# Adding and transposing transfers that wait for each other, in a convolution, row norm and feed-forward kernel whose order a planner writes

## The chip, the core and the metric

The kernel runs on one core of a Trainium2 chip. The metric is the device time of one execution in microseconds (us), lower is better: the median of three executions. A profile comes from one more execution. The engines are TensorE (PE, matrix products; PEld, its weight loads), VectorE (DVE), ScalarE (ACT), GpSimd (POOL) and SyncE (SP, which here only issues transfers). Sixteen DMA engines move data; transfers are issued from the queues of SP, POOL and, at the start, ACT.

## What is computed

The input x is 8 sequences of 4224 tokens of 192 numbers. First each token gets, for each of 8 heads, a softmax over 7 weights, and the weighted sum of itself and the six tokens ahead of it; then a row norm; then two products with a ReLU between; and the sum with the convolution's result is the output. In the reference's words, shortened:

```python
w = exp(weight_gen - max(weight_gen, -1)); w = w / (sum(w, -1) + 1e-09)
x_unf = x_pad[:, arange(S)[:, None] + arange(K)[None, :], :].reshape(B, S, K, H, group)
y = einsum('bshk,bskhg->bshg', w, x_unf).reshape(B, S, D)
mu = mean(y, -1); var = mean((y - mu) ** 2, -1)
yn = (y - mu) / sqrt(var + 1e-06) * g_ln
out = y + maximum(yn @ w_ch1, 0.0) @ w_ch2        # 192 -> 768 -> 192
```

## The kernel before

The 33792 tokens lie as 128 partitions of 264 tokens each. They are worked off in chunks of 4 or 6 tokens a partition (convolution), in parts of 4, 8 or 12 (row norm) and in groups of 4 (products): 51 chunks, 29 parts, 66 groups.

Softmax of a stretch: maxima on VectorE, subtraction on GpSimd (L333), exponentials on ScalarE, sums and the weights' product on VectorE into the PSUM tile wn.

Convolution of a chunk, `conv`: VectorE makes the seven products of x and wn, two taps at a time into tiles `pr` (five of them) and one into `y` (L395). Two of the `pr` tiles are then added up, half to half, by a transfer that accumulates in SBUF, issued from GpSimd: `dma_add` (L401), the *adding* transfer, 102 in all. GpSimd sums the rest into y with four additions (`add`, L398).

Row norm of a part, `norm`: ScalarE makes the sums and squares (L439, L444) and the root, VectorE a Newton step (L472 to L478), ScalarE the scaled rows `xh` (L490). For each group of 4 tokens ScalarE writes the fp16 half of xh into `hl` (L506) and GpSimd the rest of the split (L508). SP then issues a transposing transfer from `hl` into `xT` (L512), 66 in all: the *transposing* transfer. There are two hl tiles and three xT tiles; ScalarE may write an hl again when the transposing transfer that reads it has landed, and SP may issue the next transposing transfer into an xT when TensorE has read the one before.

Products of a group: three units of 256 hidden channels, each with 16 wide products and its share of the narrow ones, with which two units fill one stretch (L522); ScalarE evicts with a ReLU (L552), VectorE makes the low half (L554); 72 products of the second layer (L591 to L593) follow and VectorE adds them to y (L604). SP stores y (L611), and loads x (L302) and the softmax weights (L308).

Nothing of this is ordered by a scheduler at run time. `Plan.order` lists all operations once: each has an engine, a planned cost, operations that it depends on, and a due time `want` (its token, less a number from the table WANT). It picks, among the engines, the operation that may start earliest, with operations that are due first preferred within AHEAD ns, and none that is due more than WINDOW after the oldest that is left. Transfers share one planned pipe (`dma_free`), with a cost of their own each: `dma=3300.0 * n / 6` for an adding one, 2700 for a transposing one, and `dma_ns` for the rest. Each engine then runs its own list strictly in that order. An instruction that waits holds everything behind it on its engine, and on SP and GpSimd that goes for transfers' issues too.

Of the kernel before, what the change touches and what calls it, by code (L numbers as in the profile page):

```python
# [12 lines left out]
ALU = mybir.AluOpType  # L13
# [3 lines left out]
P = 128  # L17
# [6 lines left out]
CHUNK = 6  # L24
# [4 lines left out]

WANT = {'load': 38.75, 'wload': 44.01, 'max': 26.33, 'sub': 29.98, 'exp': 31.81, 'sum': 24.37,  # L30
    'rcp': 22.57, 'inv': 22.65, 'mul': 24.16, 'conv': 21.21, 'step': 0.73, 'dma': -2.14, 'add':
    -1.02, 'sums': 11.85, 'squares': 7.05, 'rstd': 13.07, 'newton': 9.37, 'xh': 6.82, 'lo':
    11.91, 'relu': 3.64, 'hlo': 0.84, 'narrow': 3.27, 'o0': -2.91, 'o1': -4.07, 'o2': -3.07,
    'o3': -3.06, 'final': -0.48}
W_WANT = {'load': 35.41, 'a': 15.24, 'c': 21.99, 's1': 17.87, 'load2': 9.56, 'c2': 13.77, 's2':
    3.7}
FIRST = {'soft': 1.2, 'conv': 7.09, 'norm': 7.75}
AHEAD = 58.5
WINDOW = 12.5

# [8 lines left out]
class Op:  # L49
    __slots__ = ("rank", "eng", "cost", "want", "fn", "lat", "dma", "deps", "nxt", "left", "ready",  # L50
                 "bufs", "start", "end")


class Plan:
# [10 lines left out]

    def op(self, eng, cost, want, fn, r=(), w=(), lat=120.0, dma=0.0):


        o = Op()
        o.rank, o.eng, o.cost, o.want, o.fn, o.lat, o.dma = len(self.ops), eng, cost, want, fn, lat, dma  # L70
        o.deps, o.nxt, o.ready, o.start, o.end = set(), [], 0.0, None, None
        o.bufs = []
        for k in (*r, *w):
# [17 lines left out]
    def order(self):  # L91
        tenant = {p: [None] * len(t) for p, t in self.pools.items()}
        free, cand, dma_free, out = {}, {}, 0.0, []
        for o in self.ops:
            o.left = len(o.deps)
            for d in o.deps:
                d.nxt.append(o)
            cand.setdefault(o.eng, [])
            free[o.eng] = 0.0
            if not o.left:  # L100
                cand[o.eng].append(o)
# [10 lines left out]
        def earliest(o):  # L112
            t = max(free[o.eng], o.ready)
            for b in o.bufs:
                if b.slot is None:
                    v = vacant(b) if b.ops[0] is o else None
                    if v is None:
                        return None
                    t = max(t, v[0])
            return t  # L120

        by_want, lead = sorted(self.ops, key=lambda o: o.want), 0
        while len(out) < len(self.ops):
# [21 lines left out]
            if o.dma:  # L145
                dma_free = max(t + o.cost + self.DMA_START[o.eng], dma_free) + o.dma
                o.end = dma_free + self.DMA_END
            cand[o.eng].remove(o)
            for x in o.nxt:
# [9 lines left out]
def kernel(  # L159
# [72 lines left out]
    def dma_ns(n):  # L232
        return n * P / 280.0

# [43 lines left out]

    def sp(want, fn, r, w, dma):
        op("SP", 450, want, fn, r=r, w=w, dma=dma)  # L280

# [79 lines left out]
    def conv(c):  # L361
# [38 lines left out]
        def dma_add(to, k):  # L400
            Q.dma_start(flat(to), flat(k), accum_op=ALU.add, max_dma_last_dim=CHUNK * D * 4)  # L401

# [13 lines left out]
        for i, k in enumerate((1, 3)):  # L416
            op("Pool", 900, c0 + 2 * i * st + WANT["dma"], lambda k=k: dma_add(k, k + 1), [(prs[k], 1)],
               [(prs[k], 0)], dma=3300.0 * n / 6)
        for i, (k, h) in enumerate(((5, 0), (5, 1), (1, 0), (3, 0))):
# [9 lines left out]
    def norm(pa):  # L429
# [53 lines left out]
        for g in range(0, n, NT):  # L483
# [18 lines left out]
            def pairs(xh):  # L502
# [9 lines left out]
               lambda hl=hl, xT=xT: SY.dma_start_transpose(at(xT), at(hl).rearrange("p t a d -> p (t a d)")),  # L512
               [(hl, 0), (hl, 1)], [xT], 2700.0)

# [283 lines left out]
    for t in range(NT):  # L798
        output(prev, t, C - WANT[f"o{t}"])
    for o in plan.order():  # L800
        o.fn()

# [29 lines left out]
```

## Time and profile before

| | |
|---|---|
| median of 3 executions | 920.84 us (918.64 to 921.96) |
| the profiled execution | 925.24 us, its span 923.5 us |
| mean granted clock of TensorE | 0.979 of 2.4 GHz |
| busy: PE, DVE, POOL, ACT | 824.6, 789.4, 696.9, 674.8 us |
| transfers on SP's queue | 47.6% of the 16 DMA engines' span |
| transfers on GpSimd's queue | 31.5% |
| waits of ScalarE's hl (L506) for xT's transfer | 23.4 us, 4 times, at most 12.3 |

The span runs from the first instruction to the last; the profiled execution's own time has 1.74 us around it. An engine's busy time is that of its instructions, DMA issues of SP and semaphores not among them. The clock is the share of TensorE's cycles that was granted: 1.0 is 2.4 GHz, and its other level is 1.2 GHz, so 0.9 over a stretch means that it was at the lower level for a fifth of it. The DMA share is the mean of 16 engines and can pass 1 in a stretch, since a packet counts where it starts. "To landing" runs from a transfer's issue to its last byte.

### The profile page before, as it was taken

How to read it: one execution, taken by the hardware profiler on the slowest of the kernel's cores; microseconds unless marked ns; L12 is line 12 of the kernel's file. 1: busy time of each engine (PE TensorE's matmuls, PEld its weight loads, DVE VectorE, ACT ScalarE, POOL GpSimd, SP SyncE). 2: the span in 40 equal slices, each digit the busy share in tenths (PEclk: the TensorE clock that was granted, in tenths of full speed). 3: DMA queues.
4: the chain of work that ended last, by engine and by line, in shares of the span. 5: the costliest groups of instructions: out<-in, count | busy, mean ns of one | idle time of the engine just before them, and what ended most of it. 6: DMA issues, size and time to landing. Idle time of an engine off the chain costs nothing.

```text
span 923.5 us, 21518 instructions
## 1 busy us (share of the span) xinstructions
PE 824.6 (89%) x8716; PEld 734.4 (80%) x8716; DVE 789.4 (85%) x833; ACT 674.8 (73%) x1773; POOL 696.9 (75%) x403
## 2 busy tenths in 40 slices
PE   0047898999999999999999995999999999899997
PEld 0036786988888898879989885988889888789997
DVE  6998997999999989999999895898989989774442
ACT  2687785897968788878886884878787789487421
POOL 3798997999879888797797793889779788783100
PEclk9989998999999999999999997999999999899999
DMA  9966869998997988996989879879988876951411
GB/s 225 225 116 140 204 137 153 186 180 162 195 189 146 176 180 143 173 186 158 192 129 207 183 106 124 196 159 142 199 170 137 182 167 124 114 124 47 78 53 53
DMA packets 137995, 142.23 MB, mean 154 GB/s; under 512 B 107495, under 2 KB 108903, under 8 KB 137895
## 3 DMA queue, kind: packets, MB, share of 16 engines
q1 hardware_dynamic: 122983, 88.95, 47.6%
q0 software_dynamic: 14688, 51.91, 31.5%
q8 instruction: 68, 1.11, 0.6%
q14 instruction: 32, 0.26, 0.1%
q10 hardware_dynamic: 224, 0.00, 0.0%
HBM read 36.43 MB, written 25.95 MB: 68 GB/s over the span
## 4 chain that ended last, share of the span: by engine, by line
DVE 29%; PE 25%; ACT 8%; POOL 7%; DMA 6%; issue 6%; DVEq 0%; POOLq 0%; ACTq 0%
DVE pr L395 14%; PE ph L522 12%; DVE hlo L554 7%; DMA xT<-hl 6%; POOL y L398 5%; PE po L591 4%; PE po L593 4%; PE po L592 4%; DVE y L395 2%; DVE y L604 2%; ACT hh L552 2%; ACT xh L490 2%; ACT junk L439 2%; ACT hl L506 1%; POOL hl L508 1%
## 5 line engine op out<-in xcount | busy, mean ns | idle before, releaser
L398 POOL TENSOR_TENSOR y<-y,pr 128x1152 f32<-128x1152 f32 (+1 forms) x204 | 498.7, 2469 | 72.6 <-DVE pr L395 69.3
L591 PE MATMUL po<-c_w2h,hh 128*128 128x192 f16 x1584 | 391.6, 247 | 0.0
L593 PE MATMUL po<-c_w2h,hlo 128*128 128x192 f16 x1584 | 391.1, 247 | 0.0
L592 PE MATMUL po<-c_w2l,hh 128*128 128x192 f16 x1584 | 391.1, 247 | 0.0
L522 PE MATMUL ph<-xT,c_w1h 128*128 128x256 f16 x2376 | 333.0, 277 | 37.6 <-DMA xT<-hl 20.3
L395 DVE TENSOR_TENSOR pr<-x,wn 128x2304 f32<-128x2304 f32 (+1 forms) x153 | 338.4, 2217 | 4.8 <-DMA x<-in_x_dram 2.6
L522 PEld LDWEIGHTS <-c_w1h 128*128 128x128 f16 x2376 | 230.2, 99 | 78.0 <-issue 41.7
L554 DVE SCALAR_TENSOR_TENSOR hlo<-ph,hh 128x1024 f16<-128x1024 f32 x198 | 238.9, 1219 | 55.0 <-ACT hh L552 54.6
L552 ACT ACTIVATE hh<-ph 128x1024 f16<-128x1024 f32 x198 | 200.0, 1012 | 94.5 <-PE ph L522 61.1
L522 PE MATMUL ph<-xT,c_w1l 128*128 128x256 f16 (+1 forms) x1584 | 214.3, 277 | 16.3 <-DVE hlo L554 16.0
L591 PEld LDWEIGHTS <-hh 128*128 128x128 f16 x1584 | 155.5, 98 | 12.4 <-issue 10.7
L508 POOL TENSOR_TENSOR hl<-xh,hl 128x768 f16<-128x768 f32 x66 | 113.2, 1715 | 60.7 <-ACT hl L506 60.3
L592 PEld LDWEIGHTS <-hh 128*128 128x128 f16 x1584 | 155.6, 98 | 1.9
L593 PEld LDWEIGHTS <-hlo 128*128 128x128 f16 x1584 | 155.6, 98 | 0.1
L522 PEld LDWEIGHTS <-c_w1l 128*128 128x128 f16 (+1 forms) x1584 | 109.6, 97 | 51.3 <-issue 31.4
L490 ACT ACTIVATE xh<-y,s 128x192 f32<-128x192 f32 x264 | 123.9, 536 | 31.0 <-DVE s L478 31.0
L444 ACT ACTIVATE junk<-y,s 128x192 f32<-128x192 f32 x264 | 119.3, 452 | 6.1
L401 POOL DMA_DIRECT2D pr<-pr x102 | 97.5, 964 | 28.8 <-DVE pr L395 26.3
L604 DVE SCALAR_TENSOR_TENSOR y<-po,c_fs,y 128x384 f32<-128x384 f32 x132 | 80.4, 611 | 44.1 <-PE po L593 44.0
L439 ACT ACTIVATE junk<-y 128x192 f32<-128x192 f32 x264 | 95.2, 361 | 29.2 <-POOL y L398 23.1
L506 ACT ACTIVATE hl<-xh 128x768 f16<-128x768 f32 x66 | 54.9, 832 | 23.5 <-DMA xT<-hl 23.4
L395 DVE TENSOR_TENSOR y<-x,wn 128x1152 f32<-128x1152 f32 (+1 forms) x51 | 60.3, 1182 | 0.3
(62 smaller groups left out, 333.3 us busy)
## 6 DMA issues: line engine op xcount, KB each, us to landing
pr<-pr POOLq DMA_DIRECT2D x60, 576.0 KB, 6.7
x<-in_x_dram SPq DMA_DIRECT2D x30, 576.0 KB, 8.5
out_dram<-y SPq DMA_DIRECT2D x30, 576.0 KB, 4.5
pr<-pr POOLq DMA_DIRECT2D x42, 384.0 KB, 6.4
out_dram<-y SPq DMA_DIRECT2D x21, 384.0 KB, 4.6
x<-in_x_dram SPq DMA_DIRECT2D x20, 384.0 KB, 8.5
w<-in_weight_gen_dram SPq DMA_DIRECT2D x21, 336.0 KB, 8.4
pr<-in_moe_w_ch_dram SPq DMA_DIRECT2D x1, 1152.0 KB, 7.2
```

Of the source, the lines that this page charges most:

```text
L395: V.tensor_tensor(out=ov, in0=xv, in1=wv, op=ALU.mult)
L398: E.tensor_tensor(out=flat(0), in0=flat(0), in1=flat(k), op=ALU.add)
L439: A.activation(junk, at(y)[:, j, :], AF.Identity, scale=-1.0 / D, accum_out=at(s4)[:, 3, t : t + 1])
L444: A.activation(junk, at(y)[:, j, :], AF.Square, bias=at(s4)[:, 3, t : t + 1], accum_out=at(s4)[:, 0, t : t + 1])
L490: A.activation(at(xh)[:, t, :], at(y)[:, i, :], AF.Identity, bias=at(s4)[:, 3, g + t : g + t + 1], scale=at(s4)[:, 1, g + t : g + t + 1])
L508: lambda xh=xh, hl=hl: Q.tensor_tensor(out=halves(hl, True), in0=pairs(xh), in1=halves(hl, False), op=ALU.subtract),
L522: T_.matmul(at(gp["ph"][u])[:, r, v * 2 * P : (v + 1) * 2 * P], W[w][rows, wb, (2 * u + v) * P : (2 * u + v + 1) * P], xv[rows, r, xb, :, ...
L552: lambda: A.activation(at(hh)[:, us, :], at(ph), AF.Relu), [ph], [(hh, u)])
L554: lambda: V.scalar_tensor_tensor(out=at(hlo)[:, us, :], in0=at(ph), scalar=0.0, in1=at(hh)[:, us, :], op0=ALU.max, op1=ALU.subtract),
L591: T_.matmul(o, tok(hh, j), w2h[:, j, :], start=(j == 0), stop=False)
L592: T_.matmul(o, tok(hh, j), w2l[:, j, :], start=False, stop=False)
L593: T_.matmul(o, tok(hlo, j), w2h[:, j, :], start=False, stop=(j == NF - 1))
```

## The change

Two kinds of transfers are marked: the adding ones ("add") and the transposing ones ("turn"). In the plan, a transfer of one kind starts no sooner than the planned end of the last one of the other kind; and in the program it waits on the landing of the last one of the other kind that stands ahead of it in the plan (`behind`, `add_manual_dep`). Transfers of one kind may still overlap each other, and loads and stores are not touched. The planned costs change (transfers cheaper, the issue of a transposing one dearer), and so do the due times, AHEAD and WINDOW. The work is the same.

```diff
--- before.py
+++ after.py
@@ -27,16 +27,16 @@
 TINY = struct.unpack("<f", struct.pack("<I", (1023 - 126) << 20))[0]
 
 
-WANT = {'load': 38.75, 'wload': 44.01, 'max': 26.33, 'sub': 29.98, 'exp': 31.81, 'sum': 24.37,
...
-AHEAD = 58.5
-WINDOW = 12.5
+WANT = {'load': 38.96, 'wload': 44.01, 'max': 25.94, 'sub': 29.98, 'exp': 32.11, 'sum': 24.37,
...
+AHEAD = 55.78
+WINDOW = 20.72
 
 
 class Buf:
@@ -48,7 +48,7 @@
 
 class Op:
     __slots__ = ("rank", "eng", "cost", "want", "fn", "lat", "dma", "deps", "nxt", "left", "ready",
-                 "bufs", "start", "end")
+                 "bufs", "start", "end", "kind", "behind")
 
 
 class Plan:
@@ -63,12 +63,13 @@
     def pool(self, name, tiles):
         self.pools[name] = tiles
 
-    def op(self, eng, cost, want, fn, r=(), w=(), lat=120.0, dma=0.0):
+    def op(self, eng, cost, want, fn, r=(), w=(), lat=120.0, dma=0.0, kind=None):
 
 
         o = Op()
         o.rank, o.eng, o.cost, o.want, o.fn, o.lat, o.dma = len(self.ops), eng, cost, want, fn, lat, dma
         o.deps, o.nxt, o.ready, o.start, o.end = set(), [], 0.0, None, None
+        o.kind, o.behind = kind, None
         o.bufs = []
         for k in (*r, *w):
             b = k[0] if isinstance(k, tuple) else k
@@ -91,6 +92,8 @@
     def order(self):
         tenant = {p: [None] * len(t) for p, t in self.pools.items()}
         free, cand, dma_free, out = {}, {}, 0.0, []
+
+        last, clear = {"add": None, "turn": None}, {"add": 0.0, "turn": 0.0}
         for o in self.ops:
             o.left = len(o.deps)
             for d in o.deps:
@@ -111,6 +114,8 @@
 
         def earliest(o):
             t = max(free[o.eng], o.ready)
+            if o.kind:
+                t = max(t, clear[o.kind])
             for b in o.bufs:
                 if b.slot is None:
                     v = vacant(b) if b.ops[0] is o else None
@@ -145,6 +150,10 @@
             if o.dma:
                 dma_free = max(t + o.cost + self.DMA_START[o.eng], dma_free) + o.dma
                 o.end = dma_free + self.DMA_END
+            if o.kind:
+                other = "turn" if o.kind == "add" else "add"
+                o.behind, last[o.kind] = last[other], o
+                clear[other] = max(clear[other], o.end)
             cand[o.eng].remove(o)
             for x in o.nxt:
                 x.left -= 1
@@ -230,7 +239,7 @@
         return 100 + 2.16 * n
 
     def dma_ns(n):
-        return n * P / 280.0
+        return n * P / 370.0
 
 
     A.preload_act_table_set("natural_log_exp_and_others")
@@ -276,8 +285,8 @@
     def xkey(t, back=False):
         return ("x", "h") if back else ("x", t % RING)
 
-    def sp(want, fn, r, w, dma):
-        op("SP", 450, want, fn, r=r, w=w, dma=dma)
+    def sp(want, fn, r, w, dma, kind=None):
+        op("SP", 1400 if kind else 450, want, fn, r=r, w=w, dma=dma, kind=kind)
 
     def load_x(ch):
         t0, n = ch["S"], ch["n"]
@@ -398,7 +407,7 @@
             E.tensor_tensor(out=flat(0), in0=flat(0), in1=flat(k), op=ALU.add)
 
         def dma_add(to, k):
-            Q.dma_start(flat(to), flat(k), accum_op=ALU.add, max_dma_last_dim=CHUNK * D * 4)
+            return Q.dma_start(flat(to), flat(k), accum_op=ALU.add, max_dma_last_dim=CHUNK * D * 4)
 
         nd = n * D
         for i, k in enumerate((1, 3, 0, 5)):
@@ -415,7 +424,7 @@
             return
         for i, k in enumerate((1, 3)):
             op("Pool", 900, c0 + 2 * i * st + WANT["dma"], lambda k=k: dma_add(k, k + 1), [(prs[k], 1)],
-               [(prs[k], 0)], dma=3300.0 * n / 6)
+               [(prs[k], 0)], dma=3000.0 * n / 6, kind="add")
         for i, (k, h) in enumerate(((5, 0), (5, 1), (1, 0), (3, 0))):
             op("Pool", q_ns(nd), c0 + (4 + 2 * i) * st + WANT["add"], lambda k=k, h=h: add(k + h),
                [(prs[k], h)], yw)
@@ -510,7 +519,7 @@
                [(xh, 0), (xh, 2), (hl, 0)], [(hl, 1)])
             sp(S0 + g - WANT["lo"] + 0.5,
                lambda hl=hl, xT=xT: SY.dma_start_transpose(at(xT), at(hl).rearrange("p t a d -> p (t a d)")),
-               [(hl, 0), (hl, 1)], [xT], 2700.0)
+               [(hl, 0), (hl, 1)], [xT], 1900.0, "turn")
 
 
 
@@ -797,8 +806,11 @@
         products(a, b)
     for t in range(NT):
         output(prev, t, C - WANT[f"o{t}"])
+    made, apart = {}, mybir.DependencyInfo(mybir.DependencyClass.Sync, mybir.DependencyReason.DATA)
     for o in plan.order():
-        o.fn()
+        made[o] = o.fn()
+        if o.behind:
+            tc.add_manual_dep(made[o].ins, made[o.behind].ins.name, apart, reason="transfers kept apart")
 
 
 # ---- launch: one core; inputs and outputs as the reference has them ----
```

The lists of all engines are written anew. Lines stand 9 further down in the new file from `order` on (L398, L401, L508 and L512 are L407, L410, L517 and L521). In brackets are the semaphores that an instruction waits for: DMAHW is a transfer of SP, DMASW one of GpSimd.

The first place is GpSimd's list around the splits of groups 40 and 41 (the rows with hl). Before:

```order
L401 DMA pr_76<-pr_76 128x1152 [waits DVE_49]
L398 TENSOR_TENSOR y_74<-y_74,pr_77 128x1152 [waits DMASW4_49,Pool_49]
L333 TENSOR_TENSOR e_96<-w_65,mx_92 128x672 [waits DMAHW5_49,DVE_49]
L398 TENSOR_TENSOR y_74<-y_74,pr_79 128x1152 [waits DMASW5_49,Pool_49]
L508 TENSOR_TENSOR hl_84<-xh_82,hl_84 128x2x384 [waits DMAHW5_49,Activation_49]
L401 DMA pr_78<-pr_78 128x1152 [waits DVE_49]
L508 TENSOR_TENSOR hl_83<-xh_81,hl_83 128x2x384 [waits DMAHW6_49,Activation_49]
L398 TENSOR_TENSOR y_75<-y_75,pr_80 128x1152 [waits DMAHW0_49,DVE_49]
```

After:

```order
L407 TENSOR_TENSOR y_74<-y_74,pr_80 128x1152 [waits DMAHW3_49,DVE_49]
L407 TENSOR_TENSOR y_74<-y_74,pr_80 128x1152 [waits Pool_49]
L410 DMA pr_77<-pr_77 128x1152 [waits DVE_49]
L407 TENSOR_TENSOR y_74<-y_74,pr_78 128x1152 [waits DMASW4_49,Pool_49]
L517 TENSOR_TENSOR hl_84<-xh_82,hl_84 128x2x384 [waits DMAHW6_49,Activation_49]
L517 TENSOR_TENSOR hl_83<-xh_81,hl_83 128x2x384 [waits Activation_49]
L407 TENSOR_TENSOR y_74<-y_74,pr_79 128x1152 [waits DMASW5_49,Pool_49]
L407 TENSOR_TENSOR y_75<-y_75,pr_80 128x1152 [waits DVE_49]
L410 DMA pr_76<-pr_76 128x1152 [waits DMAHW5_49]
L407 TENSOR_TENSOR y_75<-y_75,pr_80 128x1152 [waits Pool_49]
```

Before, an adding transfer stands right behind the split of group 40 and waits for VectorE alone. Now one stands ahead of that split, the two splits follow each other, two sums come, and the next adding transfer waits for an SP transfer (DMAHW5), the transposing one of group 41.

The second place is SP's list at the same groups (xT_85 takes group 40). Before:

```order
L611 DMA out_dram<-y_69 16x8x1152 [waits DMAHW1_49,DVE_49]
L512 DMA_TRANSPOSE xT_85<-hl_84 128x12x128 [waits DMAHW2_49,PE_49,Pool_49]
L302 DMA x<-in_x_dram 128x1x1152 [waits DMAHW3_49]
L308 DMA w_64<-in_weight_gen_dram 128x1x672 [waits DMAHW4_49]
L512 DMA_TRANSPOSE xT_86<-hl_83 128x12x128 [waits DMAHW5_49,PE_49,Pool_49]
L512 DMA_TRANSPOSE xT_87<-hl_84 128x12x128 [waits DMAHW6_49,PE_49,Pool_49]
```

After:

```order
L620 DMA out_dram<-y_69 16x8x1152 [waits DMAHW3_49,DVE_49]
L521 DMA_TRANSPOSE xT_85<-hl_84 128x12x128 [waits DMAHW4_49,DMASW6_49,DMAHW5_49,PE_49,Pool_49]
L521 DMA_TRANSPOSE xT_86<-hl_83 128x12x128 [waits DMAHW6_49,PE_49,Pool_49]
L311 DMA x<-in_x_dram 128x1x1152 [waits DVE_49]
L311 DMA x<-in_x_dram 128x1x1152 [waits DMAHW7_49]
L317 DMA w_65<-in_weight_gen_dram 128x1x672 [waits DMAHW0_49]
```

The transposing transfer of group 40 now also waits for an adding one (DMASW6), and that of group 41 follows it at once; the loads of x and w, which stood between the two, stand behind both.

The third place is GpSimd's list behind the split of group 42. Before:

```order
L508 TENSOR_TENSOR hl_84<-xh_82,hl_84 128x2x384 [waits DMAHW2_49,Activation_49]
L401 DMA pr_77<-pr_77 128x1152 [waits DVE_49]
L398 TENSOR_TENSOR y_75<-y_75,pr_78 128x1152 [waits DMASW7_49,Pool_49]
L401 DMA pr_79<-pr_79 128x1152 [waits DVE_49]
L398 TENSOR_TENSOR y_67<-y_67,pr_80 128x1152 [waits DMAHW1_49,DVE_49]
```

After:

```order
L517 TENSOR_TENSOR hl_84<-xh_82,hl_84 128x2x384 [waits DMAHW4_49,Activation_49]
L410 DMA pr_78<-pr_78 128x1152 [waits DVE_49]
L407 TENSOR_TENSOR y_75<-y_75,pr_77 128x1152 [waits DMASW6_49,Pool_49]
L410 DMA pr_79<-pr_79 128x1152 [waits DVE_49]
L407 TENSOR_TENSOR y_75<-y_75,pr_76 128x1152 [waits DMASW7_49,Pool_49]
L342 TENSOR_TENSOR e_97<-w_66,mx_93 128x672 [waits DMAHW7_49]
L407 TENSOR_TENSOR y_67<-y_67,pr_80 128x1152 [waits DMAHW3_49,DVE_49]
L407 TENSOR_TENSOR y_67<-y_67,pr_80 128x1152 [waits Pool_49]
```

In both, two adding transfers stand behind the split with a sum between them. Now the transposing transfer that reads hl_84 stands behind both in the plan and waits for the second of them.

## Rows read from the trace of the kernel before

**Rows 1.** page, whole span: busy time and share of the span by engine
```profile
PE 824.6 (89%) x8716; PEld 734.4 (80%) x8716; DVE 789.4 (85%) x833; ACT 674.8 (73%) x1773; POOL 696.9 (75%) x403
```
**Rows 2.** stages: stretch, us, busy PE PEld DVE ACT POOL, clock, DMA share, GB/s
```profile
60.00:170.00 110.00, 91.92 (x915) 78.87 (x916) 99.09 (x121) 85.01 (x231) 98.12 (x67) 0.92 0.78 150
170.00:400.00 230.00, 224.71 (x2419) 201.10 (x2417) 220.75 (x224) 190.35 (x508) 203.44 (x116) 1.00 0.94 178
400.00:425.00 25.00, 22.73 (x231) 20.02 (x230) 22.94 (x19) 16.20 (x50) 21.65 (x13) 0.93 0.90 177
...
540.00:570.00 30.00, 20.40 (x216) 17.77 (x214) 18.03 (x17) 16.61 (x42) 19.18 (x11) 0.90 0.99 109
570.00:770.00 200.00, 198.42 (x2116) 177.69 (x2115) 184.97 (x175) 158.25 (x423) 159.80 (x84) 0.99 0.84 164
770.00:805.00 35.00, 31.80 (x315) 28.12 (x313) 27.94 (x30) 24.82 (x62) 30.52 (x18) 0.90 0.92 118
```
**Rows 3.** the longest pieces of the chain: start us, us, what
```profile
544.61 20.21 DMA xT<-hl
...
630.15 10.77 DMA xT<-hl
...
779.08 13.76 DMA xT<-hl
```
**Rows 4.** ACT in order of time: start us, us, [idle before, releaser]
```profile
564.84 0.84 ACT L506 ACTIVATE hl<-xh 128x768 f16<-128x768 f32 x1 [12.31 <-DMA xT<-hl]
```
**Rows 5.** tiles xT and pr: us from issue to landing, all transfers of each
```profile
DMA to landing us min/median/max: 3.2/6.1/20.2
...
DMA to landing us min/median/max: 3.8/6.6/20.8
```
**Rows 6.** issues from 544, 743 and 732: count, KB each, us to landing
```profile
pr<-pr POOLq DMA_DIRECT2D x1, 576.0 KB, 20.8
xT<-hl SPq DMA_TRANSPOSE x1, 20.2
...
x<-in_x_dram SPq DMA_DIRECT2D x1, 384.0 KB, 4.2
xT<-hl SPq DMA_TRANSPOSE x2, 3.2
...
pr<-pr POOLq DMA_DIRECT2D x2, 576.0 KB, 5.1
```
**Rows 7.** two stretches as in rows 2: transposing beside adding, adding alone
```profile
547.00:556.00 9.00, 9.00 (x100) 8.09 (x98) 7.92 (x10) 4.64 (x13) 8.26 (x4) 1.00 1.24 62
770.00:774.70 4.70, 4.70 (x54) 4.48 (x52) 4.53 (x9) 3.98 (x8) 4.70 (x4) 1.00 0.79 189
```
**Rows 8.** groups by line and form: xcount, busy us, mean ns, idle us before
```profile
L398 POOL TENSOR_TENSOR y<-y,pr 128x1152 f32<-128x1152 f32 x120 | 330.1, 2751 | 65.8 <-DVE pr L395 63.3
...
L508 POOL TENSOR_TENSOR hl<-xh,hl 128x768 f16<-128x768 f32 x66 | 113.2, 1715 | 60.7 <-ACT hl L506 60.3 <-POOL hl L508 0.2
L395 DVE TENSOR_TENSOR pr<-x,wn 128x1536 f32<-128x1536 f32 x63 | 109.4, 1747 | 4.2 <-DMA x<-in_x_dram 2.6 <-DVE wn L349 0.5 <-issue 0.5
L401 POOL DMA_DIRECT2D pr<-pr x102 | 97.5, 964 | 28.8 <-DVE pr L395 26.3 <-DVE wn L472 0.8 <-issue 0.7
...
L333 POOL TENSOR_TENSOR e<-w,mx 128x672 f32<-128x672 f32 x21 | 33.7, 1606 | 0.4 <-DVE mx L331 0.4
...
L663 DVE TENSOR_SCALAR po<-pr 128x384 int32<-128x384 int32 x3 | 1.6, 553 | 0.0
```
**Rows 9.** waits on SP's queue: engine line, waited for, us, times, longest
```profile
SPq L512 <- POOL hl L508: 187.5, 38, 16.8
SPq L512 <- PE ph L522: 71.7, 16, 10.6
```
**Rows 10.** waits of TensorE between 60 and 170
```profile
PEld L522 <- DMA xT<-hl: 5.2, 2, 4.4
PE ph L522 <- DMA xT<-hl: 4.5, 2, 4.2
```

More of the change, by code (lines that the diff above doesn't have):

```diff
@@ L27 @@
 TINY = struct.unpack("<f", struct.pack("<I", (1023 - 126) << 20))[0]
-WANT = {'load': 38.75, 'wload': 44.01, 'max': 26.33, 'sub': 29.98, 'exp': 31.81, 'sum': 24.37,
[L31 to L37, printed above, removed]
-AHEAD = 58.5
-WINDOW = 12.5
+WANT = {'load': 38.96, 'wload': 44.01, 'max': 25.94, 'sub': 29.98, 'exp': 32.11, 'sum': 24.37,
+    'rcp': 22.52, 'inv': 22.65, 'mul': 20.53, 'conv': 21.5, 'step': 0.73, 'dma': -2.12, 'add':
+    -0.96, 'sums': 13.68, 'squares': 6.77, 'rstd': 16, 'newton': 9.52, 'xh': 6.97, 'lo': 12.06,
+    'relu': 3.79, 'hlo': 2.89, 'narrow': 4.16, 'o0': -3.05, 'o1': -3.95, 'o2': -2.9, 'o3': -3.5,
+    'final': 0.14}
+W_WANT = {'load': 32.14, 'a': 16.41, 'c': 17.44, 's1': 17.99, 'load2': 9.41, 'c2': 13.47, 's2':
+    -0.78}
+FIRST = {'soft': -3.62, 'conv': 8.03, 'norm': 0.14}
+AHEAD = 55.78
+WINDOW = 20.72
 class Buf:
```

## The prediction

> **What bounds the kernel.** I read the page first, then the stages, the chain of waits, and the transfers. The page shows TensorE busy for 824.6 of 923.5 us and VectorE for 789.4 [rows 1]; the DMA engines' share is 0.78 to 0.99 in the stages. By stages TensorE is the limit from 60 us on. Between 170 and 400 it starts 2419 matmuls in 230 us, 10.52 a us, and between 570 and 770 2116 in 200, 10.58; the reader should take these as its full pace. Four stages fall short of 10.52 a us [rows 2]: 60 to 170 by 242 matmuls (23.0 us), 400 to 425 by 32 (3.0 us), 540 to 570 by 100 (9.5 us), 770 to 805 by 53 (5.1 us). In the last three the granted clock is 0.93, 0.90 and 0.90, so part of each loss is time at the lower of its two levels after TensorE stood.
>
> The chain names a cause for the two largest of the middle: it rests 20.21 us on one transposing transfer from 544.61 and 13.76 us on one from 779.08 [rows 3]. What follows is on ScalarE: the next fp16 split (L506) stands 12.31 us because the buffer hl is still being read by that transfer [rows 4]; ScalarE runs in order, so the evictions behind it are late, and TensorE is out of work. Two shorter pieces of 10 to 11 us, one of which is shown (from 630.15, 10.77 us), lie in the stage with the full pace [rows 2, 3]. So a transposing transfer costs TensorE nothing up to about 10.8 us, and something from 13.8 on.
>
> Why is one so long? A transposing transfer lands after 3.2 us at best and 6.1 in the median; an adding one after 3.8 and 6.6 [rows 5]. The 20.2 us one was issued 0.4 us after an adding one, which took 20.8; two transposing transfers beside an x load took 3.2 each, two adding ones without a transposing one 5.1 [rows 6]. From 547 to 556, with both kinds under way, the DMA engines show a share of 1.24 and move 62 GB/s; with adding alone 0.79 and 189 GB/s [rows 7]. Together the two kinds do not share the engines, they hold each other up.
>
> **The change, part by part.** The sum goes against the profiled execution, 925.24 us (span 923.5 and 1.74 around it); the median of the runs is 920.84, 4.4 below.
>
> *What goes: the jams.* Apart, the worst order of one adding and one transposing transfer is 5.1 + 3.2 = 8.3 us, under 10.8. So 540 to 570 gives back 9.5 us and 770 to 805 5.1. Of the 3.0 at 400 I take half, 1.5: no long transfer stands on the chain there. Of the 23.0 between 60 and 170 I take 4.5, TensorE's own waits for xT; its weight loads waited another 5.2 [rows 10], and the rest is supply from VectorE, busy 99.09 of those 110 us [rows 2]. Together -20.6. Bounds: 0, if something else is late at the same places, and -40.6, all four stages at full pace.
>
> *What is added on GpSimd.* By the order, 31 of the 102 adding transfers now name a transposing one, and GpSimd runs in order: the y sums, the next hl split and the softmax subtraction are queued behind, and VectorE's products wait for the pr buffers that the sums free. From the end of the split that feeds a transposing transfer to its landing is 3.2 us and the 0.1 until its issue. Counted by the durations of rows 8 (2.75 us a y sum, 1.72 a split, 0.96 an issue; small sums shorter), the order has 4.2 us or more of GpSimd work in between at 30 of the 31 places, and 2.6 at one. So nearly nothing, if SP issues at once. It does not always: at 16 of 66 it waited for TensorE to free xT, 71.7 us in all, 10.6 at most [rows 9]. 31/66 of that would now stand on GpSimd, 34 us, the upper bound. But GpSimd has 26.6 us idle between 170 and 400 and 40.2 between 570 and 770 [rows 2], and such a wait means that the producers are ahead. I take +2, nearer the cover than the bound. Below nothing there is no case: a wait can't shorten GpSimd's own work.
>
> *What is added on SP.* 32 of the 66 transposing transfers now wait for an adding one; behind them in SP's queue stand x and w loads and the stores of y. VectorE's products waited 2.6 us in all for x [rows 8], so loads have room. At 13 places the adding transfer stands behind the split or ends less than 1 us ahead of it, so the transposing one is issued up to 5.1 us late and lands 8.3 us after the split; at six of them, spread over the run, two adding ones stand there, the second 0.96 + 2.75 = 3.7 us later, or 5.2 with a softmax subtraction of 1.6 between [rows 8]. There the transposing one lands 3.7 + 5.1 + 3.2 = 12.0 or 13.5 us after the split, between the 10.8 that cost nothing and the 13.8 that cost 5.1. But the order has some 25 us of GpSimd work there until the next split into the same buffer, so I take +3 for all. Bounds: 0 and 6 x 5.1 = +31.
>
> *What is moved.* Ahead of the first row norm VectorE has the same 7 double and 3 single products, but ten more small steps of the weights' decoding at 0.55 us, so the first group comes 5.5 us later; ahead of the sixth norm one double product fewer (1.75 us earlier), ahead of the eighth one more (1.75 later) [rows 8]. I take 0 between -1.75 and +5.5. The numbers of work per engine stay as they are.
>
> *Sum.* 925.2 - 20.6 + 2 + 3 = 909.6 for a profiled execution, and 4.4 less for the median: 905 us.
>
> **A rule that speaks against it.** The Trainium skill ("DMA: Bandwidth & Descriptors", Issuing engines are not separate DMA queues) says that transfers of all queues run on the same 16 engines and interleave; and in its Rules for kernel authors that a transposing transfer next to ordinary ones needs nothing. If they only interleaved, keeping them apart would change their order and not their total, the first rival below. The rate of 62 GB/s beside 189 in rows 7 does not agree.
>
> **Rivals.**
> *Nothing is gained.* The bytes take their share of the engines in any order, and the late group of one jam is late elsewhere. For it: the engines are at a share of 0.94 between 170 and 400, at full pace all the same [rows 2]. Against it: rows 7. Time: 925.2 - 4.4 = 921.
> *Slower: the wait takes the place of the jam.* At the six places with two adding transfers ahead the transposing one lands late enough to hold hl, and ScalarE stands at its split as it did at 564.84, TensorE again at the lower clock: 6 x 5.1 = +31, with +2 on GpSimd. 925.2 - 20.6 + 33 - 4.4 = 933. It decides from the fourth such place on (4 x 5.1 = 20.4). For it: 13.5 us is close to 13.8, and the stages 60 to 400 have transfers of many kinds in flight. Against it: the 25 us of cover.
> *More is gained.* The early stage also comes to its pace, since its transfers land sooner: half of the remaining 18.5 us there and the rest of 400 to 425, -11: 894. Against it: VectorE's 99.09 of 110 us.
>
> **Numbers.** Forecast 0.60 (own range 897 to 916), nothing gained 0.11, slower 0.20, more 0.09. Two executions of one kernel differ by about 0.3%, 2.8 us. Faster than that: 0.69; the same: 0.10; slower: 0.21. The range reaches to both outer cases and leaves one in ten beyond each: 888 to 932.
>
> **What would show it.** Right: xT's landing falls to about 3.5 us in the median and stays under 10, an adding transfer's under 5.5; no stretch with a share over 1 below 100 GB/s; about 10.5 matmuls a us in every stage from 170 on, the clock at 1.00 there; ScalarE's split waits less than the present total for xT; GpSimd's waits for xT at the adding line stay below some 10 us. Wrong: such waits of tens of us with VectorE standing for pr; splits waiting 5 us and more for xT at several places; or landings that stay long, which would mean that another kind of transfer makes the jam.

## The result and the profile after

The changed kernel takes 908.10 us (median of 4 runs, 905.88 to 908.86), the kernel before 919.93 us in the same comparison (918.64 to 921.96): a ratio of 0.9865 with a 95% interval of 0.9839 to 0.9892, some 12 us faster. Ratios, here and below, leave out executions that took over 1.5% more than the fastest of their kernel, while medians hold all of them. The profiled execution took 908.86 us, with a span of 907.1. Engines, from the page:

```profile
PE 815.0 (90%) x8716; PEld 729.6 (80%) x8716; DVE 785.3 (87%) x833; ACT 676.5 (75%) x1773; POOL 696.6 (77%) x403
```

The same work as in [rows 1], with less standing around it. The stages of [rows 2], with 0 to 60 and 425 to 540 besides; columns as there:

```profile
0.00:60.00 60.00, 1.17 (x4) 1.03 (x5) 46.27 (x73) 27.19 (x75) 34.30 (x29) 1.00 0.81 198
60.00:170.00 110.00, 94.20 (x926) 80.13 (x926) 102.25 (x125) 90.45 (x243) 104.97 (x71) 0.94 0.77 163
170.00:400.00 230.00, 225.70 (x2441) 203.26 (x2440) 217.79 (x221) 189.52 (x505) 199.79 (x115) 1.00 0.81 174
400.00:425.00 25.00, 24.39 (x266) 21.91 (x264) 24.86 (x21) 17.60 (x51) 22.64 (x12) 1.00 0.83 183
425.00:540.00 115.00, 113.07 (x1220) 101.60 (x1219) 104.11 (x107) 93.76 (x250) 91.22 (x49) 1.00 0.79 167
540.00:570.00 30.00, 29.39 (x322) 26.38 (x320) 29.85 (x25) 21.38 (x53) 27.32 (x16) 1.00 0.90 185
570.00:770.00 200.00, 197.21 (x2134) 177.60 (x2133) 183.59 (x179) 164.25 (x430) 162.15 (x85) 1.00 0.73 158
770.00:805.00 35.00, 33.02 (x358) 29.59 (x357) 32.48 (x32) 24.00 (x71) 30.77 (x20) 1.00 0.62 117
```

Two stages of before that were not shown:

```profile
0.00:60.00 60.00, 6.94 (x42) 4.69 (x42) 50.69 (x77) 30.25 (x84) 38.84 (x32) 1.00 0.83 200
...
425.00:540.00 115.00, 114.48 (x1241) 103.15 (x1239) 107.82 (x107) 95.64 (x255) 95.61 (x51) 1.00 0.82 170
```

Add up the counts of matmuls from top to bottom (one that lies on the edge of two rows counts in both). Up to 400 us it is 3371 after and 3376 before: on balance nothing is gained there. By 805 it is 7671 against 7495, so 176 more, 16.7 us at 10.52 a us; the profiled executions differ by 16.4. Of these 106 come in 540 to 570, 43 in 770 to 805 and 35 in 400 to 425; the clock there is at 1.00, where it was 0.90 to 0.93.

The landings of xT and of pr after, us (minimum, median, maximum), against [rows 5]:

```profile
DMA to landing us min/median/max: 3.2/3.5/8.0
...
DMA to landing us min/median/max: 3.8/6.4/16.9
```

The 16.9 is a load of weights at the start into the same tile; where the trace shows a landing, no transfer of one kind overlaps one of the other any more. The transposing transfers land sooner; the adding ones hardly do, with 6.4 us in the median against 6.6, where the prediction's sign for being right asked for under 5.5. ScalarE's splits, whose group waited 23.4 us for such transfers before (one of these waits in [rows 4]), idle 0.3 us in all (the group's last column):

```profile
L515 ACT ACTIVATE hl<-xh 128x768 f16<-128x768 f32 x66 | 55.0, 833 | 0.3
```

And the added waits, from the waits by line (us in total, times, longest), beside those of [rows 9]:

```profile
SPq L521 <- DMA pr<-pr: 157.1, 24, 13.7
...
SPq L521 <- POOL hl L517: 53.6, 29, 3.6
...
SPq L521 <- PE ph L531: 19.1, 3, 10.6
...
POOL pr L410 <- DMA xT<-hl: 4.2, 2, 3.1
```

SP stands 157 us for adding transfers. TensorE waits for xT at two places, both before 100 us, 11.9 us in all; without the added waits (first experiment) it is 12.6 us, so SP's standing does not show in TensorE's waits. The chain of waits of this trace reaches back from the end to 705.73 us only, and holds no transfer from there on; for the stage at 540, where before a piece of 20.21 us stood [rows 3], it says nothing.

### The profile page after: what moved, and what is told of

It reads as the page before. It is cut to its first block, busy times and chain, and to the rows that moved or that the text cites. A ratio compares the mean times of both kernels' runs of the same rounds, so it can differ in the third digit from the quotient of the medians.

```text
span 907.1 us, 21485 instructions
## 1 busy us (share of the span) xinstructions
PE 815.0 (90%) x8716; PEld 729.6 (80%) x8716; DVE 785.3 (87%) x833; ACT 676.5 (75%) x1773; POOL 696.6 (77%) x403
## 5 line engine op out<-in xcount | busy, mean ns | idle before, releaser
L407 POOL TENSOR_TENSOR y<-y,pr 128x1152 f32<-128x1152 f32 (+1 forms) x204 | 506.0, 2516 | 71.4 <-DVE pr L404 66.4
L531 PE MATMUL ph<-xT,c_w1h 128*128 128x256 f16 x2376 | 328.8, 275 | 26.0 <-DVE hlo L563 19.3
L531 PEld LDWEIGHTS <-c_w1h 128*128 128x128 f16 x2376 | 227.3, 99 | 69.9 <-issue 45.0
L531 PE MATMUL ph<-xT,c_w1l 128*128 128x256 f16 (+1 forms) x1584 | 210.2, 274 | 7.3 <-DMA xT<-hl 5.8
L517 POOL TENSOR_TENSOR hl<-xh,hl 128x768 f16<-128x768 f32 x66 | 117.1, 1809 | 26.2 <-ACT hl L515 24.3
L410 POOL DMA_DIRECT2D pr<-pr x102 | 100.6, 1043 | 33.9 <-DVE pr L404 25.4
L613 DVE SCALAR_TENSOR_TENSOR y<-po,c_fs,y 128x384 f32<-128x384 f32 x132 | 77.6, 608 | 17.3 <-PE po L602 17.3
## 6 DMA issues: line engine op xcount, KB each, us to landing
pr<-in_moe_w_ch_dram SPq DMA_DIRECT2D x1, 1152.0 KB, 16.9
```

What stands on the lines that cost most here:

```text
L407: E.tensor_tensor(out=flat(0), in0=flat(0), in1=flat(k), op=ALU.add)
L410: return Q.dma_start(flat(to), flat(k), accum_op=ALU.add, max_dma_last_dim=CHUNK * D * 4)
L517: lambda xh=xh, hl=hl: Q.tensor_tensor(out=halves(hl, True), in0=pairs(xh), in1=halves(hl, False), op=ALU.subtract),
L531: T_.matmul(at(gp["ph"][u])[:, r, v * 2 * P : (v + 1) * 2 * P], W[w][rows, wb, (2 * u + v) * P : (2 * u + v + 1) * P], xv[rows, r, xb, :, ...
```

## Experiments

T is a transposing transfer, A an adding one. "Overlaps" are the T that lay beside an A for over 2 us, counted from issues and landings. All ratios are to the kernel before, run on the same chip with each group. Each kernel was traced once, and in each trace 51 to 61 of the 66 T have a landing (51 of them in [rows 5]), so overlaps and longest landings are those of these T.

| kernel | median us | ratio (95%) | overlaps | longest landing of xT, us |
|---|---|---|---|---|
| before | 919.9 | 1 | 32 | 20.2 |
| after | 908.1 | 0.9865 (0.9839 to 0.9892) | 0 | 8.0 |
| new order, no waits | 908.4 | 0.9888 (0.9862 to 0.9913) | 10 | 11.2 |
| old order, waits | 981.4 | 1.0688 (1.0659 to 1.0718) | 0 | 7.4 |
| after, old due times | 901.0 | 0.9809 (0.9785 to 0.9833) | 0 | 7.4 |
| the same, no waits | 902.5 | 0.9829 (0.9800 to 0.9858) | 21 | 18.2 |
| before, new due times | 914.1 | 0.9913 (0.9882 to 0.9944) | 27 | 18.4 |
| new costs and times, no rule, no waits | 913.2 | 0.9935 (0.9911 to 0.9960) | 28 | 13.9 |
| before, four hl | 911.2 | 0.9911 (0.9878 to 0.9944) | 34 | 23.0 |
| before, no stores | 910.6 | 0.9898 (0.9858 to 0.9938) | 40 | 13.5 |
| before, stores in SBUF | 909.1 | 0.9888 (0.9845 to 0.9930) | 31 | 13.3 |

**The new order without the waits.**

```diff
     for o in plan.order():
         made[o] = o.fn()
-        if o.behind:
+        if False and o.behind:
             tc.add_manual_dep(made[o].ins, made[o.behind].ins.name, apart, reason="transfers kept apart")
```

> The changed kernel's order, with the 63 added waits left out: the work and each engine's list are those of the changed kernel. Theory A (keeping the two kinds apart is what pays; the order only makes room for the waits): SP's queue waited 157 us at 24 places for adding transfers; without that those transposing transfers go out beside an adding one, jams are back, xT lands after 5 to 7 us in the median and 15 to 20 at most, and the time lies between 913 and 925 us, nearer to the 920 of before than to the 908 of the changed kernel. Theory B (the new order alone pays, the jams were a sign and not the cause): 906 to 910 us, whatever the landings do.

908.4 us, the changed kernel's time; the two intervals lie over each other. Ten overlaps are back and the longest landing is 11.2 us, but the splits' group idles 0.3 us as with the waits. So theory B holds for the time: the waits, as instructions, give nothing here. What jams cost this run does not tell, since they did not come back to the 15 to 20 us of theory A.

**The waits without the new order.** The transfers are marked with their kind as in the changed kernel (not shown), and then:

```diff
+    last, apart = {}, mybir.DependencyInfo(mybir.DependencyClass.Sync, mybir.DependencyReason.DATA)
     for o in plan.order():
-        o.fn()
+        made = o.fn()
+        if o.kind:
+            other = last.get("turn" if o.kind == "add" else "add")
+            if other is not None:
+                tc.add_manual_dep(made.ins, other.ins.name, apart, reason="transfers kept apart")
+            last[o.kind] = made
```

> The order of before, with the waits alone added (each adding or transposing transfer waits for the last one of the other kind ahead of it in the old plan). Theory A: no transfer of one kind lies beside one of the other, xT lands after about 3.3 us in the median and under 9 at most, the loss of 9.5 us at 540 to 570 and of 5.1 at 770 to 805 is gone; since the old plan made no room for the waits, some of GpSimd's adding transfers wait, 5 to 15 us in all, so 905 to 915 us. Theory B: 918 to 922 us or, where the waits hold up GpSimd, up to 935.

981.4 us, 7% slower, beyond what either theory allowed, though the landings are as short as theory A had them. Its waits and a piece of its chain (start us, us, what):

```profile
SPq L513 <- DMA pr<-pr: 348.9, 41, 17.1
...
POOL pr L402 <- DMA xT<-hl: 77.8, 19, 6.9
```

```profile
279.81 3.20 DMA xT<-hl
...
283.55 8.56 DMA pr<-pr
...
292.25 3.85 DMA xT<-hl
```

Here the chain is set by transfers that take turns: one T, then an A behind it, then the next T. GpSimd works its list in order, so the y sums and splits behind an A that waits are late too, and with them the next transfer. It is a wait in the place of the jam, as the slower rival had it, though above all on GpSimd and not at ScalarE's split, which waits 3.3 us in all for T.

**The two due-time tables.** The changed kernel with the old table, and the kernel before with the new one (WANT, W_WANT, FIRST, AHEAD and WINDOW in each):

```diff
-WANT = {'load': 38.96, 'wload': 44.01, 'max': 25.94, 'sub': 29.98, 'exp': 32.11, 'sum': 24.37,
+WANT = {'load': 38.75, 'wload': 44.01, 'max': 26.33, 'sub': 29.98, 'exp': 31.81, 'sum': 24.37,
...
-AHEAD = 55.78
-WINDOW = 20.72
+AHEAD = 58.5
+WINDOW = 12.5
```

> The changed kernel with the due times, FIRST, AHEAD and WINDOW of before; waits and the planner's rule for the two kinds stay. Theory A: within 5 us of the changed kernel's 908, the two kinds apart, and since the lists ahead of the first row norm are like those of before (31.8 us of VectorE work against 39.4), the first products start some 7 us sooner than the changed kernel's 60.9 us and the time may be 2 to 3 us less: 904 to 912. Theory B: the new due times are what pays, so 915 to 922.

> The kernel of before with the new due times, FIRST, AHEAD and WINDOW alone: no waits, old planned costs, no rule for the two kinds. Theory A: adding and transposing transfers lie beside each other again as in before, xT lands after 6 us in the median and 15 to 20 at most, 913 to 930 us. Theory B: 906 to 912.

901.0 us with the old table: the fastest of all, and faster than both kernels. Its first products start sooner (42 matmuls by 60 us, after 4), yet by 400 us it has 3378 against 3371, and the rest of its lead of 77 matmuls by 805 us comes mostly in the last two stages:

```profile
570.00:770.00 200.00, 199.28 (x2163) 179.81 (x2161) 187.23 (x183) 162.54 (x422) 166.84 (x89) 1.00 0.80 167
770.00:805.00 35.00, 35.00 (x382) 31.74 (x381) 33.75 (x35) 29.34 (x82) 32.92 (x21) 1.00 0.65 125
```

So the expected reason (the start) is wrong, though the time is inside the expected range. The new table alone, without rule, costs or waits, brings 914.1 with the overlaps still there; its runs lie from 903.1 to 923.6. Both theories told part of it. Note that its splits no longer wait for T, although one T still lands after 18.4 us (the last number is the idle time ahead of the 66 splits, in us):

```profile
L506 ACT ACTIVATE hl<-xh 128x768 f16<-128x768 f32 x66 | 54.9, 831 | 0.2
```

So another order alone can take away the wait for hl, without keeping the two kinds apart.

**The old table without the waits, and the new costs and table without the planner's rule.** The first is the kernel of 901.0 us with the edit of the first experiment. The second is the changed kernel with that edit and with the rule taken out of the planner:

```diff
             t = max(free[o.eng], o.ready)
-            if o.kind:
-                t = max(t, clear[o.kind])
```

> The kernel of 901 us (the changed kernel with the due times, FIRST, AHEAD and WINDOW of before) with the added waits left out; the planner's rule and costs stay, and every engine's list is the same. Theory P (the rule alone pays; where it is in the plan the waits are idle): 899 to 903 us, with ten or so short overlaps and no landing over 11.5 us. Theory A (waits are needed where the slack is as small as in the old due times, a hlo of 0.84 against 2.89): jams of 12 us and more at some places, 904 to 912.

> The changed kernel without the waits and without the planner's rule that a transfer of one kind starts no sooner than the planned end of the last of the other; the new planned costs and due times stay. Theory P (the rule pays, since it thins out the jams): transfers of the two kinds lie beside each other as often as in before (27 or more transposing ones for over 2 us), landings up to 15 to 20 us, 912 to 920 us. Theory Q (the new costs and due times pay): 906 to 910.

The first takes 902.5 us; the interval overlaps that with waits. But theory P's short overlaps are not what one finds: there are 21 overlaps and eight landings over 11 us, one of 18.2 for a transfer issued at 415.78. TensorE hardly notices. From 400 to 425 it is at full pace; from 425 to 540 it starts 1205 matmuls, where the kernel with the waits starts 1223 (1.7 us more):

```profile
400.00:425.00 25.00, 25.00 (x272) 22.14 (x270) 23.50 (x19) 20.75 (x62) 20.38 (x10) 1.00 0.97 139
425.00:540.00 115.00, 111.57 (x1205) 100.39 (x1203) 104.81 (x102) 91.63 (x237) 91.08 (x50) 1.00 0.98 176
```

The second takes 913.2 us with 28 overlaps, as theory P had it. From it to the new order without waits (908.4) only the rule is added: 0.9935 to 0.9888, about 4 us, with intervals that just touch. Every new list of orders tried is faster than the one of before, whatever was changed in the plan; with one order for each setting, it is not shown how much of a step is the rule's and how much comes with any other order.

**Four hl tiles in the kernel before.** Every list as before, the tile that a split goes into taken in turn from four.

```diff
     def at(b):
+        if b.pool == "hl":
+            i = seen.setdefault(b, len(seen) % 4)
+            return (plan.pools["hl"] + spare)[i]
         return plan.pools[b.pool][b.slot]
```

> The kernel of before, every engine's list the same, with the hl tiles in turn in four buffers in place of two, so that ScalarE's split waits for no transposing transfer. If a jam costs through the held hl buffer, as the prediction's step on the jams had it (ScalarE waits 23.4 us in all, TensorE runs out behind it): those 23.4 us fall to nothing, 540 to 570 and 770 to 805 lose less than half of their 9.5 and 5.1 us, 908 to 913 us. If it costs through the late xT itself (TensorE waits 20.6 us for it), the jams stay and so does the time: 916 to 921.

911.2 us, and ScalarE's splits wait for no T any more, while the landings are longer than ever (23.0 us). The two stages:

```profile
540.00:570.00 30.00, 21.64 (x217) 18.79 (x215) 20.38 (x18) 16.69 (x47) 17.99 (x11) 0.89 1.13 103
770.00:805.00 35.00, 35.00 (x381) 31.30 (x380) 33.60 (x34) 26.33 (x77) 33.80 (x22) 1.00 0.99 148
```

The second is at full pace with its jams (landings of 12.1 and 11.9 us, before 13.8 and 13.0). The first is as short of work as before, against the expectation that it would lose less than half: its T lands after 23.0 us, and the chain goes from there straight to TensorE, without ScalarE between:

```profile
541.83 23.04 DMA xT<-hl
564.92 0.61 PE ph L528 x4
```

So a late landing costs in two ways, through the held hl and, when it is late enough, by itself. Which of the two weighs more this experiment does not tell: it brings 8 us, and nothing of the largest loss.

**What makes a jam.** In the kernel before, the jam at 544 was not one of two transfers only. The loads that SP issued in it, from 548.75 and 550.19 on, landed late as well (KB, us to landing):

```profile
x<-in_x_dram SPq DMA_DIRECT2D x1, 576.0 KB, 18.1
w<-in_weight_gen_dram SPq DMA_DIRECT2D x1, 336.0 KB, 17.5
```

What starts it was looked for in three small programs, each run once, and two edits of the kernel before. First the pairs in a program of their own:

```diff
+    phases = (("tAlone", (T,)), ("aAlone", (Ad,)), ("cAlone", (Cq,)), ("lAlone", (Lq,)),
+              ("ta", (T, Ad)), ("tc", (T, Cq)), ("tl", (T, Lq)), ("ac", (Ad, Cs)), ("al", (Ad, Ls)),
```

> A separate small program, none of the kernel's work in it: a transposing transfer (T, 128x1536 fp16 from SBUF to SBUF), an adding one (A, 128x1152 fp32, 576 KB), a plain copy in SBUF of the size of A (C) and a load of that size from DRAM (L), each alone and in pairs issued together, six times each, with nothing else under way. Alone, all theories: T 3.2 us to landing, A 3.8 to 5. Theory J1 (the adding and the transposing kind hold each other up): T with A lands after 8 to 20 us for both, T with C or L after less than 6, A with C or L after less than 8. Theory J2 (two transfers of SBUF to SBUF hold each other up whatever they do): T with C is as slow as T with A. Theory J3 (they only share the engines): T with A is done after the sum, some 7 to 8 us, as is every other pair.

Inconclusive: the rounds of different phases ran into each other, so "alone" is not alone in it (T "alone" up to 7.7 us). The second program ties every round to the landings of the round before and sets the distances by VectorE:

```diff
+    ("ta", "A0 T0.4"), ("to", "O0 T1.9"), ("ao", "O0 A1.5"), ("tao", "O0 A1.5 T1.9"),
+    ("tal", "L0 A1.5 T1.9"), ("tco", "O0 C1.5 T1.9"), ("tao2", "O0 A1 T2.5"),
```

> A separate small program: the transfers of the kernel alone, in pairs and in threes, six rounds each, every round behind the landing of all before it, with set distances between the issues (a store O of 576 KB from SBUF to DRAM, an adding transfer A 1.5 us later, a transposing one T 0.4 us after that, as the kernel before has them at 542.71, 544.23 and 544.61). Theory S (a jam needs three: the adding and the transposing transfer held back behind a store, so that both start together): T with A lands after 4 to 8 us, T with O after 4 to 7, T with A behind O after 10 us or more. Theory L (any third transfer does it): T with A behind a load L is as slow. Theory C (the adding is not needed): T with a plain copy behind O is as slow. Theory E (it takes the engines' work on SBUF beside it): no pair and no three is over 9 us here.

Issues by their destination, with the median us to landing (ta holds three distances, T behind A by 0.2, 1.3 and 2.3 us; tao two; the letter behind the underscore is the transfer):

```profile
ta_A<-src POOLq DMA_DIRECT2D x18, 576.0 KB, 5.3
tao_A<-src POOLq DMA_DIRECT2D x12, 576.0 KB, 6.4
...
a_A<-src POOLq DMA_DIRECT2D x6, 576.0 KB, 4.8
...
ta_T<-hl SPq DMA_TRANSPOSE x18, 5.8
tao_T<-hl SPq DMA_TRANSPOSE x12, 7.1
t_T<-hl SPq DMA_TRANSPOSE x6, 3.7
...
tal_T<-hl SPq DMA_TRANSPOSE x6, 7.8
```

No jam: T beside A lands after 5.8 us, behind a store as well after 7.1, 8.4 at most behind a load. Theories S, L and C fall, E was left. Then two edits of the kernel before, whose lists stay:

```diff
-               lambda: SY.dma_start(tokens(out, t0, n), at(y)[:, :n, :].rearrange("p t d -> p (t d)")),
+               lambda: SY.dma_start(tokens(out, t0, n) if t0 + n == C else sink[:, : n * D], at(y)[:, :n, :].rearrange("p t d -> p (t d)")),
```

(the other issues no store but the last)

> The kernel of before, every engine's list the same, without the stores of y but the last (50 of 51 are left out, so most of the output is not written). Theory S (a store beside the two kinds makes the jam): no xT lands after more than 11 us, 540 to 570 and 770 to 805 are at full pace, 903 to 910 us. Theory E or any that does not need the store: landings of 12 us and more stay, 913 to 921 us.

> The kernel of before, with each store of y but the last put into one unused SBUF tile in place of DRAM: as many bytes from the same queue at the same places (most of the output is not written). If it is the write to DRAM that makes the jam, as without stores: 903 to 911 us and no landing over 11 us. If it is any third transfer on SP's queue: landings of 12 to 20 us as in before, 913 to 921 us.

910.6 and 909.1 us. The landings of xT in the two, and the stage from 540 with the stores in SBUF:

```profile
DMA to landing us min/median/max: 3.2/6.5/13.5
```

```profile
DMA to landing us min/median/max: 3.2/6.0/13.3
```

```profile
540.00:570.00 30.00, 29.79 (x321) 26.77 (x319) 27.82 (x23) 22.20 (x63) 23.81 (x14) 1.00 1.05 183
```

The overlaps stay (40 and 31) and the landings of 15 to 20 us are gone, also where as many bytes are written to SBUF from the same queue. With the order of before, then, the writes to DRAM have a part in the worst jams. They are not the only way to be rid of these: the new costs and table without the rule, with all stores to DRAM, show no landing over 13.9 us. Landings of 13 us remain in both, against the 11 that the theory allowed, 540 to 570 is not quite at full pace without stores (308 matmuls), and ScalarE's splits still wait 16.1 and 14.3 us for T, 23.4 before. A good part of the gain lies elsewhere, from 60 to 170, where the kernel before starts 915 matmuls; without stores, and with stores in SBUF:

```profile
60.00:170.00 110.00, 95.01 (x971) 82.51 (x971) 104.43 (x125) 90.00 (x251) 103.48 (x70) 0.95 0.73 142
60.00:170.00 110.00, 95.87 (x974) 82.77 (x975) 104.43 (x125) 90.05 (x250) 103.60 (x70) 0.94 0.80 161
```

Last, the sequence of the jam at 544 with the engines at work:

```diff
+SEQ = "O0 A1.5 T1.9 L6 W7.5 U8.2"
+    ("seqs", SEQ, "S"), ("seqp", SEQ, "P"), ("seqvq", SEQ, "VQ"), ("seqall", SEQ, "VQSP"),
```

> A separate small program: the pair (A, then T 0.4 us later) and the sequence of the kernel before from 542.71 on (a store O of 576 KB to DRAM, A at +1.5, T at +1.9, a load of x at +6, one of softmax weights at +7.5, a second T, called U, at +8.2 us), each with the other engines at rest, and with them at work: VectorE at products 128x1536, GpSimd at sums 128x1152, ScalarE at splits 128x768, TensorE at 256-column products, one by one and all together; six rounds each. In the kernel T landed after 20.2 us here. Theory E (the engines' work on SBUF makes the jam): at rest T lands after 7 to 9 us, with one of the engines, or with all, after 12 us or more. Theory M (it takes more transfers, no work): T of the sequence lands after 12 us or more at rest already. Neither: all under 10 us, and what makes 20.2 of it in the kernel stays open.

```profile
pair_T<-hl SPq DMA_TRANSPOSE x6, 6.1
pairall_T<-hl SPq DMA_TRANSPOSE x6, 6.7
seq_T<-hl SPq DMA_TRANSPOSE x6, 7.1
...
seqv_T<-hl SPq DMA_TRANSPOSE x6, 7.5
...
seqall_T<-hl SPq DMA_TRANSPOSE x6, 7.3
```

T lands after 8.6 us at most. (With VectorE and GpSimd both at work, the loads came later than set, so the whole sequence is tested with each engine alone.) Neither theory holds. Why the same T took 20.2 us in the kernel and about 7 here stays open; shown is only that neither the pair nor this sequence suffices, and that, in the order of before, the stores to DRAM have a part in it.

## Why the prediction was right, and where it was not

*The jams.* The three later stages came out much as counted: 540 to 570 gave 106 matmuls or 10.1 us (forecast 9.5), 770 to 805 43 or 4.1 (5.1), 400 to 425 35 or 3.3 (1.5). xT's landings went to 3.5 us in the median and 8.0 at most, under the 8.3 of the worst order. The path through the held hl, on which the prediction built, is borne out at 770 to 805, where four hl tiles bring full pace; at 540 to 570 they bring nothing, since TensorE waits for the late xT itself.

*60 to 170, and what is moved.* The prediction took 4.5 us of TensorE's waits for xT as a gain here, and the moved work as 0. The gain was there: nearly all of these 4.5 us is one wait at 145.98 (the row below), and it is gone, with 289 matmuls from 140 to 170 in place of 255 (3.2 us). But what the new order moves ate it. The first product starts at 60.91 us in place of 51.00, 9.9 us later, where 5.5 was the prediction's upper bound, and by 140 us the changed kernel is 61 matmuls behind (5.8 us). The stretches 0 to 140 and 140 to 170, before and after, and the rows of TensorE, two before and one after:

```profile
0.00:140.00 140.00, 73.09 (x705) 61.62 (x706) 125.61 (x169) 95.52 (x262) 113.09 (x82) 0.96 0.79 174
140.00:170.00 30.00, 25.78 (x255) 21.94 (x253) 24.18 (x29) 19.75 (x53) 23.88 (x17) 0.89 0.81 138
...
0.00:140.00 140.00, 68.29 (x644) 57.59 (x645) 118.85 (x166) 91.35 (x246) 109.27 (x79) 0.95 0.78 176
140.00:170.00 30.00, 27.08 (x289) 23.57 (x287) 29.67 (x33) 26.28 (x73) 30.00 (x21) 1.00 0.81 172
```

```profile
51.00 1.44 PE L522 MATMUL ph<-xT,c_w1h 128*128 128x256 f16 x6 [16.06 <-DMA xT<-hl]
...
145.98 1.46 PE L522 MATMUL ph<-xT,c_w1h 128*128 128x256 f16 x6 [4.22 <-DMA xT<-hl]
...
60.91 1.44 PE L531 MATMUL ph<-xT,c_w1h 128*128 128x256 f16 x6 [6.20 <-DMA xT<-hl]
```

By 400 us the two are level. The later start is not the whole account: the kernel with the old table starts as early as before, and it has only 3378 by 400 us. But the stretch does allow more, as the two kernels with the order of before and no stores to DRAM show, with 56 and 59 matmuls more than before from 60 to 170 (5.3 and 5.6 us). The stages that were put down as at full pace gave 2.1 (170 to 400) and 1.7 us (570 to 770), and 425 to 540 lost 21 matmuls, 2.0 us.

*The added waits.* GpSimd's waits for xT are 4.2 us in all, and SP's for adding transfers 157, but as time they cost nothing: 908.1 us with them, 908.4 without. So neither the +2 nor the +3 is there. (The 5.2 us of its step on SP is 5.3 by the durations that it names, which changes nothing.) In the old order the same waits cost over 60 us; the forecast was safe because it counted them in the new order, where the rule had moved the A behind the T that they name.

*The sum.* The forecast was 905 us, 897 to 916, and 908.1 was measured. The 909.6 for a profiled execution is within 1 us of the 908.86 measured, and that is partly luck: the 4.5 us of 60 to 170 that did not stay, and the 5 us of added waits that did not come, cancel.

*The step that failed is the last one,* "4.4 less for the median". After the change profile and median lie 0.8 us apart, and the medians differ by 12 us, not by 16. The profile is one execution: in the nine other kernels of the table that were traced, it lies between 4.6 us below and 1.7 above its kernel's median. So the 4.4 belonged to one execution of the kernel before, and had no place in the forecast for another kernel. Whether it was longer jams that made that execution slow is not shown, since only this one was traced. The ratio forecast, 0.983, is just below the measured interval.

*What was credited wrongly.* The prediction let keeping the two kinds apart on the chip give the gain. The gain is the order's: without the waits it is the same, with the old table even where landings reach 18.2 us. By the ratios without waits, rule and costs with the old table give 16 us, the new table alone 8; together they give 10, so the new table, under the rule, costs 6 us, and 7 with the waits (908.1 against 901.0). And "something from 13.8 on" is no property of the transfer: with the old table and no waits, landings of 17 and 18 us go with a time that is 1.5 us longer than with waits, and the splits waited 3.4 us in all for the buffer. Nor do the two kinds always hold each other up: alone, A and T are both done 7.0 us after the first issue, less than the 4.8 + 3.7 of one after the other. There the rule that transfers interleave (the Trainium skill, "DMA: Bandwidth & Descriptors", Issuing engines are not separate DMA queues) agrees; in the kernel's stretch of [rows 7] interleaving alone does not account for the 62 GB/s. The other rule that the prediction takes from the Trainium skill ("DMA: Bandwidth & Descriptors", Rules for kernel authors), that a transposing transfer next to ordinary ones needs nothing, stands there in a row on transposes that corrupt each other's data and does not speak of time.

## What to carry to other kernels

A transfer that is late costs what waits for its buffers: look first for the engine that wants the source tile back, and try more buffers or another order before adding waits. If two transfers are to be kept apart, put it into the planned order and not into a wait on the chip alone: where the plan did not know of them, the same waits made this kernel 7% slower. Count what a new order moves as carefully as what it mends: here a later start took back what the early stage had gained. And work out the gain against the median run: one profiled execution can lie several us from it, and the next kernel's will not lie there by as much.

## What was not expected of the hardware

An adding transfer of 576 KB and a transposing one, which took 20.8 and 20.2 us together in the kernel, take 5.3 and 5.8 us as a pair with nothing else beside it, and 5.5 to 5.9 and 7.0 to 7.5 us behind a store with one engine at work. Two loads issued in the midst of that jam took 18.1 and 17.5 us. Turning the stores of the kernel from DRAM to SBUF brings the longest landing from 20.2 to 13.3 us, in one trace of each, and the median time from 919.5 to 909.1 us. The cause of the jam is not found.
